# Moving the second quad's queries and keys from GpSimd's casting loads to a hardware queue, more of the early casts to VectorE, and holding GpSimd's loads back

## The chip, the cores and the metric

The kernel runs on one core of one Trainium2 chip. The metric is the time of one execution in device microseconds. A core has TensorE (PE in the profile; its weight loads are PEld), VectorE (DVE), ScalarE (ACT), GpSimd (POOL) and SyncE (SP), and 16 DMA engines which all queues share. Loads issued by SyncE or ScalarE go by hardware queues, and in this kernel they bring float32 as it is into staging tiles. Loads issued by GpSimd can change the type on the way, float32 to float16. The Trainium skill states the same ("DMA: Bandwidth & Descriptors", SWDGE vs HWDGE vs iDMA: a cast during a DMA is GpSimd's alone). That is why a load moved to a hardware queue needs a cast by an engine afterwards.

## The reference

```python
batch, n_heads, seq, head_dim = (8, 12, 448, 64)        # q, k, v, float32
scores = scale * np.matmul(q, k.transpose(0, 1, 3, 2))
m = np.max(scores, axis=-1, keepdims=True)
e = np.exp(scores - m)
attn = e / (np.sum(e, axis=-1, keepdims=True) + np.exp(-m) + 1e-09)
x = attn @ v                                            # then to (3584, 768)
h = x @ w_in                                            # 768 x 2048 ("gemm1" here)
P = a[0] + a[1]*h + a[2]*h**2 + a[3]*h**3
Q = 1.0 + abs(b[0])*abs(h) + abs(b[1])*h**2
out = (P / (Q + 1e-6)) @ w_out                          # 2048 x 768 ("gemm2" here)
```

## The kernel before

Four heads of one batch entry are a "quad"; there are 3 quads per batch entry, 24 in all. For each quad the kernel transposes q and k, multiplies them (scores), takes exps on ScalarE, forms the denominators and the product with v ("attend"), and feeds gemm1, a rational function on VectorE and ScalarE, and gemm2. Batch entry 0 is done in two halves of 224 queries, so that gemm1 can start early.

The program is written as a list of operations in queues. A small planner in the kernel file simulates the engines with estimated durations and fixes each engine's static order from that. Its estimates do not run on the chip; only the order does. Three constants say when the scores of batch entry 1 and later are "due" in that plan:

```python
T0 = 18.0; T1 = 22.0; TLEAD = 5.0
def quad_due(n):
    if n < 2 * NQ:
        return T1 + 8 * P1 * (n - NQ)       # batch entry 1
    return T0 + 8 * PER * (n - NQ)          # later ones
```

Before, only quad 0 came by hardware queues, in pieces, and GpSimd's loads began at once with quad 1:

```python
def piece(ti, pr, jh, nj, dma, lat, cast, late=False):   # ti: k or q; pr: pair of heads; jh: half
    ...                                                  # one DMA into a float32 staging tile, one cast
piece(0, 0, 0, 2, "ACT", 2.8, "ACT")     # k, first pair, first half
piece(1, 0, 0, 2, "SP", 2.65, "DVE")     # q, first pair
piece(0, 0, 2, 2, "ACT", 3.4, "ACT")
piece(1, 1, 0, 2, "SP", 3.9, "DVE")
piece(0, 1, 0, 2, "ACT", 3.6, "ACT")     # k, second pair, first half
piece(0, 1, 2, 2, "SP", 3.7, "ACT")
...
kload.append(load_op(1, k, kn, "k", kfree, NN))          # GpSimd: casting load, 4 heads
qload.append(load_op(1, q, qn, "q", qfree, NN))
loads(0, "v"); loads(2, "kq"); loads(1, "v"); loads(2, "v")
ORDER = "kq3 i kq4 i kq5 v3 i v4 i v5 o kq6 o o o"       # i: a group of w_in, o: one of w_out
```

w_in comes in four groups of three GpSimd loads each. From quad 6 on, q and k are transposed by DMA instead of TensorE.

The softmax here doesn't subtract the row's maximum and nothing guards it: scores larger than these inputs give would overflow.

Of the kernel before, what the change touches and what calls it, by code (L numbers as in the profile page):

```python
# [8 lines left out]
F32 = mybir.dt.float32  # L9
# [149 lines left out]
def kernel(  # L159
# [11 lines left out]
    nc = tc.nc  # L171

    B, H, S, D = q.shape
    DM, FF = moe_w_in.shape
    J = 4
    P = S // J
# [10 lines left out]
    NE, NX, NV, NN, NK, NH, NO, NS = 12, 2, 5, 3, 6, 3, 3, 2  # L187
# [7 lines left out]
    def ring(name, n, shape, dt=F16):  # L195
# [14 lines left out]
    g_sb = ring("g", 2, [128, NFC, S])  # L210
    gx = ring("gx", 2, [128, NFC, 128])

    qn = ring("qn", NN, [P, 4, J, D])
    kn = ring("kn", NN, [P, 4, J, D])
    vn = ring("vn", NV, [P, 4, J, D])
# [19 lines left out]
    plan = Plan({  # L235
        "PE": ("att", "mm", "tr"),
        "ACT": ("head", "c0", "den", "acast", "osb", "e", "rat"),
        "DVE": ("head", "c0", "cpt", "cpt2", "mult", "cast", "wc", "ng"),
        "POOL": ("gx", "perm", "load"),
        "SP": ("x", "out"),  # L240
    }, NGEN)
# [31 lines left out]
    units += [(b, qd, 0, S) for b in range(1, B) for qd in range(NQ)]  # L273
    PER = 1.95
    DUES = (0, 0, 4, 6)
    T0 = 18.0
    T1 = 22.0
    P1 = 1.3
    LEAD = 45.0
    MB = 3  # L280
    NPE = 6
    TLEAD = 5.0
    ACM = 100

    def quad_due(n):
# [4 lines left out]
    qload, kload, vload = [], [], []  # L290
    late_cp = []
    qfree, kfree, v_free = [], [], []
# [5 lines left out]
    def load_op(n, src, dst, name, free, size):  # L298
        b, qd = divmod(n, NQ)

        def emit():
            nc.gpsimd.dma_start(
                out=dst[n % size],
                in_=src[b, 4 * qd:4 * qd + 4].rearrange("h (p j) d -> p h (j d)", j=J),
            )
        return plan.add("load", Op(
            f"ld{name}{n}", "POOL", 0.7, [hist(free, n, size)], emit,
            rel=0.0 if n < 2 * NQ else quad_due(n) - LEAD, kb=448))
# [20 lines left out]
    def first_loads():  # L329


        casts = {}
        stages = [[h_sb[0], h_sb[1]], [h_sb[2], c_sb[0]]]

        def piece(ti, pr, jh, nj, dma, lat, cast, late=False):
            src, dst = ((k, kn), (q, qn))[ti]
            eng = nc.scalar if dma == "ACT" else nc.sync
            stage = (stages[1][1 - pr] if late else stages[pr][ti]).bitcast(F32)[
                0:P, 0:2 * J * D].rearrange(
                "p (h j d) -> p h j d", h=2, j=J)[:, :, (0 if late else jh):][:, :, 0:nj]  # L340
            rows = src[0, 2 * pr:2 * pr + 2].rearrange("h (p j) d -> p h j d", j=J)
            d = plan.add("head" if dma == "ACT" else "x", Op(
                f"ld0{dma}", dma, 0.43,
                [casts[1 - pr, 1, 0], casts[1, 1, 0]] if late else [],
                lambda: eng.dma_start(out=stage, in_=rows[:, :, jh:jh + nj]),
                kb=56 * nj, lat=lat))
            out = (late_q[:, 2 * pr:2 * pr + 2] if late
                   else dst[0][:, 2 * pr:2 * pr + 2, jh:jh + nj])
            c = Op(f"c0{ti}{pr}{jh}", cast, (0.12 if cast == "DVE" else 0.2) + 0.11 * nj, [d],
                   lambda: nc.vector.tensor_copy(out=out, in_=stage) if cast == "DVE"  # L350
                   else nc.scalar.activation(out=out, in_=stage, func=AF.Copy))
            if (ti, pr, jh) != (1, 1, 0):
                plan.add("c0", c)
            for j in range(jh, jh + nj, 2):
                casts[ti, pr, j // 2] = c
        piece(0, 0, 0, 2, "ACT", 2.8, "ACT")
        piece(1, 0, 0, 2, "SP", 2.65, "DVE")
        piece(0, 0, 2, 2, "ACT", 3.4, "ACT")
        piece(1, 1, 0, 2, "SP", 3.9, "DVE")
        piece(0, 1, 0, 2, "ACT", 3.6, "ACT")  # L360
        piece(0, 1, 2, 2, "SP", 3.7, "ACT")
        for pr in range(2):
            piece(1, pr, 2, 2, "SP", 6.8, "DVE", True)
        return casts

    def loads(n, which="kqv"):
        if "k" in which:
            kload.append(load_op(n, k, kn, "k", kfree, NN))
            qload.append(load_op(n, q, qn, "q", qfree, NN))
        if "v" in which:  # L370
            vload.append(load_op(n, v, vn, "v", v_free, NV))

    def transpose_by_pe(n):

        parts, trs = [], []
        nh = 2 if n == 0 else 1
        for pr in range(2):
            ops = [[], []]
            for jh in range(nh):
                for ti, (src, dst, ld) in enumerate(((kn, kt, kload), (qn, qt, qload))):  # L380
                    un = {}
                    late = n == 0 and ti == 1 and jh == 1
                    js = range(J * jh // nh, J * (jh + 1) // nh)

                    def emit(pr=pr, un=un, src=src, js=js, late=late):
                        tp = gen[un["bank"]].bitcast(F16)
                        for j in js:
                            for hh in range(2):
                                nc.tensor.transpose(  # L389
                                    tp[64 * hh:64 * hh + 64, j * P:(j + 1) * P],  # L390
                                    late_q[:, 2 * pr + hh, j - J // 2, :] if late
                                    else src[n % NN][:, 2 * pr + hh, j, :],
                                    ident[0:P, 0:P])

                    def emit_cp(pr=pr, un=un, dst=dst, js=js):
                        c0, c1 = js[0] * P, (js[-1] + 1) * P
                        nc.vector.tensor_copy(
                            out=dst[n % NK][:, pr * S + c0:pr * S + c1],
                            in_=gen[un["bank"]].bitcast(F16)[:, c0:c1])
                    cp = Op(f"cpt{n}", "DVE", 0.1 + 0.24 / nh, [], emit_cp)  # L400
                    src_op = first_casts[ti, pr, jh] if n == 0 else ld[n]
                    tr = Op(f"t{n}", "PE", 0.4 / nh,
                            [src_op, ident_op, hist(qk_free, n, NK)], emit,
                            gen=(True, un, cp), mode="t")
                    trs.append(tr)
                    cp.deps = [tr]
                    if late:
                        late_cp.append(cp)
                    else:
                        plan.add("cpt" if n < NQ else "cpt2", cp)  # L410
                    ops[jh].append(cp)
                    tr.late = late
                    if pr == 1 and not late and (jh == nh - 1 or ti == 1):
                        (kfree, qfree)[ti].append(tr)
            if n == 0 and pr == 0:
                plan.add("cpt", first_casts[1, 1, 0])
            parts.append(ops)
        if n == 2:
            for cp in late_cp:
                plan.add("cpt", cp)  # L420
        qxp.append(None)
        kxp.append(None)
        qk_ready.append(parts)
        return trs
# [303 lines left out]
    first_casts = first_loads()  # L728
# [3 lines left out]
    ab = plan.add("x", Op("ab", "SP", 0.9, [abz], emit_ab, kb=1))  # L732
    babs_op = plan.add("head", Op("babs", "DVE", 0.2, [ab], emit_babs))

    qload.append(None)
    kload.append(None)
    ident_op = plan.add("load", Op("ident", "POOL", 0.6, [], emit_ident))
    kload.append(load_op(1, k, kn, "k", kfree, NN))
    qload.append(load_op(1, q, qn, "q", qfree, NN))
    loads(0, "v")  # L740
    loads(2, "kq")
    loads(1, "v")
    loads(2, "v")
# [18 lines left out]
    first = [op for op in trs[0] if not op.late]  # L762
    late = [op for op in trs.pop(0) if op.late]
    prev = None
    for i in range(len(units)):
        m0 = len(e_ops)
        passes = scores(i)
        nu = units[i + 1] if i + 1 < len(units) else None
        nxt = trs.pop(NQ * nu[0] + nu[1], []) if nu else []
        if nu and nu[0]:  # L770
            for op in nxt:
                op.due = quad_due(NQ * nu[0] + nu[1]) - TLEAD
                plan.add("tr", op)
            nxt = []
        more = {}
        if i == 0:
            more = {-1: first[:2], 0: first[2:4], 1: first[4:], 2: nxt[:1], 3: nxt[1:2]}
            rest = nxt[2:]
        elif i < NQ:
            more = {1: rest, 3: late if i == 2 else nxt}  # L780
            rest = []
        for op in more.get(-1, []):
            plan.add("att", op)
        for t, s in enumerate(passes):
            plan.add("att", s)
            for op in more.get(t, []):
                plan.add("att", op)
            if t == 1:
                for op in prev or []:
                    plan.add("att", op)  # L790
        prev = attend(i, m0)
# [66 lines left out]
```

## Time and profile before

| | value |
|---|---|
| time, median of 3 runs | 432.84 us (432.69 to 432.94) |
| span of the profiled run | 431.5 us (this run took 433.28 us, above all timed ones) |
| TensorE busy, 0 to 27.3 us | 18.81 of 27.3 us |
| TensorE busy, 27.3 to 60 and 60 to 120 us | all of it |
| first gemm1 matmul | 27.30 us |

First, busy time by stretches. The columns are the stretch, its length, then busy time and number of instructions for each engine, the granted TensorE clock, the DMA share and GB/s.

```profile
core 0: us, PE busy (x) PEld busy (x) DVE busy (x) ACT busy (x) POOL busy (x), PEclk, DMA share, GB/s
0.00:16.00 16.00, 8.76 (x128) 5.51 (x128) 4.66 (x28) 8.84 (x13) 9.89 (x19) 1.00 1.07 165
16.00:27.30 11.30, 10.05 (x236) 6.89 (x229) 5.88 (x21) 9.32 (x14) 6.30 (x9) 1.00 1.33 202
27.30:60.00 32.70, 32.70 (x495) 21.74 (x494) 24.29 (x44) 31.02 (x40) 15.78 (x24) 1.00 1.26 203
60.00:120.00 60.00, 60.00 (x512) 30.13 (x510) 57.20 (x80) 52.95 (x60) 27.09 (x35) 1.00 1.10 145
```

From 27.3 to 120 us TensorE has no gap, and from there to 400 us only 0.5 us, so only the head (and a tail of about 3 us) can be shortened. In the last column GpSimd's casting loads are counted by the float16 bytes they write; they read twice that. (The page of the profile has 22.35 MB for GpSimd's queue, and 45.62 MB read from memory in all.)

Next, lines of the timeline: start, duration, engine, line, operation, and in brackets the idle time before it and what ended it.

```profile
1.49 0.83 POOL L302 DMA_DIRECT2D kn<-in_k_dram  x1 [0.18 <-issue]
7.56 0.72 ACT L351 ACTIVATE kn<-h 112x256 f16<-112x256 f32 x2 [2.74 <-DMA h<-in_k_dram]
8.36 0.56 PE L472 MATMUL sps<-qt,kt 64*128 64x224 f16 x4
14.65 1.71 PE L507 MATMUL gen<-e,vn 112*32 112x224 f16 x32
20.13 0.94 PE L507 MATMUL gen<-e,vn 112*32 112x224 f16 x32
27.30 0.75 PE L573 MATMUL gen<-x,w_in 128*128 128x224 f16 x6
```

GpSimd issues its first load at 1.49 us. The last early pieces of quad 0 (k of the second pair of heads) are cast only at 7.56 us, and the scores that need them start at 8.36. The same 32 matmuls take 1.71 us at 14.65 us and 0.94 us at 20.13 us, though the granted clock column reads 1.00: TensorE runs slowly at first. ScalarE works in a fixed order: the first pair's scores are computed from 4.95 us on, but the first exp starts only at 8.19 us.

```profile
8.19 1.70 ACT L480 ACTIVATE e<-sps 112x896 f16<-112x896 f32 x2
```

The chain of waits gives the wait for that piece of k (start, duration, what):

```profile
1.72 5.82 DMA h<-in_k_dram
```

### The profile page before, as it was taken

The page shows a single profiled execution, that of the slowest core. Times are in us where ns is not written, and L with a number is a line of the kernel's source. Part 1 is how long each engine was busy: PE and PEld are TensorE (multiplying, and loading weights), DVE is VectorE, ACT ScalarE, POOL GpSimd, SP SyncE. Part 2 cuts the span into 40 slices and gives each one's busy share as a digit, 9 for nine tenths or more (in the row PEclk, how much of TensorE's full clock was granted, in tenths as well). Part 3 has the DMA queues.
Part 4 walks back from the last instruction along what each step waited for, and adds up shares of the span by engine and source line. Part 5 has one row for each costly group of instructions (what it writes and reads, how often), then busy time and mean ns, then how long its engine had stood idle before and what let it go on. Part 6 is the DMA issues. An engine that isn't in the chain of part 4 may idle for free.

```text
span 431.5 us, 8834 instructions
## 1 busy us (share of the span) xinstructions
PE 419.2 (97%) x3680; PEld 218.7 (51%) x3680; DVE 339.9 (79%) x505; ACT 327.8 (76%) x386; POOL 120.7 (28%) x172
## 2 busy tenths in 40 slices
PE   3999999999999999999999999999999999999996
PEld 2667665544444444444454444444444455555563
DVE  2445999998999887698998668979698788999800
ACT  4699999798888777888886897877798854578521
POOL 5655516566005340423703333052000000000000
PEclk9999999999999999999999999999999999999999
DMA  9999999899606947299399886373211011111132
GB/s 148 202 200 205 207 180 150 152 154 162 123 2 69 160 85 118 28 141 115 58 117 107 119 123 85 81 108 73 45 36 38 2 36 38 36 38 36 39 103 81
DMA packets 78153, 43.12 MB, mean 100 GB/s; under 512 B 36128, under 2 KB 74528, under 8 KB 78112
## 3 DMA queue, kind: packets, MB, share of 16 engines
q0 software_dynamic: 37856, 22.35, 39.7%
q1 hardware_dynamic: 39472, 19.80, 25.5%
q8 instruction: 29, 0.48, 0.5%
q10 hardware_dynamic: 784, 0.39, 0.4%
q14 instruction: 12, 0.10, 0.1%
HBM read 45.62 MB, written 11.01 MB: 131 GB/s over the span
## 4 chain that ended last, share of the span: by engine, by line
PE 89%; ACT 4%; DMA 3%; DVE 1%; issue 1%; ACTq 0%; POOLq 0%
PE gen L671 34%; PE gen L573 33%; PE gen L507 12%; PE sps L472 10%; DMA kn<-in_k_dram 2%; ACT e L480 2%; DMA h<-in_k_dram 1%; ACT c L625 1%; ACT c L628 1%; PE gen L389 1%; DVE h L590 0%; ACT lden L521 0%; DVE x L535 0%; ACT lden L523 0%; DVE c L614 0%
## 5 line engine op out<-in xcount | busy, mean ns | idle before, releaser
L480 ACT ACTIVATE e<-sps 112x896 f16<-112x896 f32 x192 | 167.1, 917 | 41.5 <-PE sps L472 41.1
L573 PE MATMUL gen<-x,w_in 128*128 128x448 f16 (+1 forms) x864 | 161.8, 332 | 0.0
L671 PE MATMUL gen<-w_out,g 128*128 128x384 f16 (+2 forms) x768 | 135.9, 326 | 0.0
L573 PEld LDWEIGHTS <-w_in 128*128 128x128 f16 x864 | 79.9, 98 | 68.3 <-issue 14.4
L671 PEld LDWEIGHTS <-g 128*128 128x128 f16 x768 | 72.7, 98 | 58.4 <-issue 10.4
L590 DVE CAST h<-gen 128x448 f16<-128x448 f32 x113 | 69.4, 618 | 24.4 <-PE gen L573 24.3
L614 DVE TENSOR_TENSOR n<-n,h 128x1792 f16<-128x1792 f16 x64 | 70.1, 1095 | 0.7
L625 ACT ACTIVATE c<-c,oneeps_c 128x1792 f16<-128x1792 f16 x32 | 57.3, 1791 | 11.4 <-DVE c L614 11.1
L472 PE MATMUL sps<-qt,kt 64*128 64x448 f16 (+1 forms) x432 | 58.4, 343 | 2.3 <-ACT e L480 1.1
L648 POOL COPY gx<-g 128x1024 f16<-128x1024 f16 x8 | 8.3, 1040 | 183.1 <-DVE g L614 183.1
L693 ACT ACTIVATE o<-gen 128x384 f32<-128x384 f32 (+2 forms) x56 | 27.4, 490 | 36.2 <-PE gen L671 36.0
L628 ACT ACTIVATE c<-c 128x1792 f16<-128x1792 f16 x32 | 54.6, 1705 | 0.3
L610 DVE TENSOR_SCALAR n<-n,abc 128x1792 f16<-128x1792 f16 x64 | 44.3, 693 | 1.1
L614 DVE TENSOR_TENSOR g<-n,c 128x1792 f16<-128x1792 f16 x32 | 35.1, 1098 | 12.8 <-ACT c L628 11.5
L433 POOL COPY kp<-kn 112x256 uint32<-112x256 uint32 x36 | 26.1, 755 | 57.2 <-DMA kt<-kp 50.3
L507 PE MATMUL gen<-e,vn 112*32 112x448 f16 (+1 forms) x864 | 41.8, 337 | 0.0
L535 DVE TENSOR_TENSOR x<-gen,lden 128x448 f16<-128x448 f32 (+1 forms) x54 | 28.3, 563 | 13.9 <-ACT lden L523 12.7
L614 DVE TENSOR_TENSOR c<-c,w 128x1792 f16<-128x1792 f16 x32 | 35.2, 1100 | 0.0
L472 PEld LDWEIGHTS <-kt 64*128 64x128 f16 x432 | 15.0, 96 | 36.5 <-issue 32.9
L507 PEld LDWEIGHTS <-vn 112*32 112x32 f16 x864 | 23.1, 99 | 14.0
L433 POOL COPY qp<-qn 112x256 uint32<-112x256 uint32 x36 | 25.2, 726 | 18.1 <-DMA qt<-qp 18.0
L610 DVE TENSOR_SCALAR n<-h,abc 128x1792 f16<-128x1792 f16 x32 | 24.7, 772 | 0.1
(42 smaller groups left out, 248.1 us busy)
## 6 DMA issues: line engine op xcount, KB each, us to landing
vn<-in_v_dram POOLq DMA_DIRECT2D x24, 224.0 KB, 8.5
kn<-in_k_dram POOLq DMA_DIRECT2D x23, 224.0 KB, 5.7
qn<-in_q_dram POOLq DMA_DIRECT2D x23, 224.0 KB, 7.4
w_in<-in_moe_w_in_dram POOLq DMA_DIRECT2D x12, 256.0 KB, 9.7
w_out<-in_moe_w_out_dram POOLq DMA_DIRECT2D x4, 768.0 KB, 16.2
out_dram<-o SPq DMA_DIRECT2D x8, 336.0 KB, 3.2
out_dram<-o SPq DMA_DIRECT2D x8, 288.0 KB, 2.8
out_dram<-o SPq DMA_DIRECT2D x7, 240.0 KB, 2.5
```

What stands on the lines that cost most here:

```text
L433: nc.gpsimd.tensor_copy(out=mid[0].bitcast(U32)[:, pr], in_=src[n % NN].bitcast(U32)[:, 2 * pr:2 * pr + 2] .rearrange("p e j d -> p j e d"))
L472: nc.tensor.matmul(out=sps[m % NS][0:(P if i == 0 and j == 1 else 128), hh, ci * qw:(ci + 1) * qw], lhsT=kt[n % NK][r, c0:c0 + (P if i == ...
L480: nc.scalar.activation(out=e_sb[m % NE], in_=sps[m % NS][0:P, :, 0:S], func=AF.Exp, scale=scale)
L507: nc.tensor.matmul(out=gen[unit["bank"]][32 * h:32 * h + 32, 0:qw], lhsT=lhs(h, j), rhs=e_sb[m % NE][:, h % 2, c0:c0 + qw], start=(j == 0) ...
L535: mult.emit = lambda s=s, uu=uu: nc.vector.tensor_tensor(out=x_sb[b % NX][:, 2 * qd + s, q0:q0 + qw], in0=gen[uu["bank"]][:, 0:qw], in1=ld ...
L573: nc.tensor.matmul(out=gen[unit["bank"]][:, fi * qw:(fi + 1) * qw], lhsT=w_in_sb[wg][:, c // 2, c % 2, (fc % FG) * 128:(fc % FG + 1) * 128 ...
L590: nc.vector.tensor_copy(out=dst, in_=src)
L610: return lambda: nc.vector.tensor_scalar(out=out, in0=in0, scalar1=s1, scalar2=s2, op0=op0, **kw)
L614: return lambda: nc.vector.tensor_tensor(out=out, in0=in0, in1=in1, op=ALU.mult)
L625: lambda: nc.scalar.activation(out=c, in_=c, func=AF.Ln, bias=oneeps_c)))
L628: lambda: nc.scalar.activation(out=c, in_=c, func=AF.Exp, scale=-1.0)))
L671: nc.tensor.matmul(out=gen[unit["bank"]][:, 0:wd], lhsT=lhs, rhs=w_out_sb[f][:, fc % FG, cols], start=(fc == 0), stop=(fc == NFC - 1))
```

## The change

The intent: the first quad's pieces should have the DMA engines to themselves, so that the exps start sooner. Quad 1's q and k also come by SyncE's queue, in four larger transfers into a part of a tile that is still unused, and VectorE casts them. VectorE also takes over the two casts of quad 0's last k pieces, which ScalarE did before. A tiny memset of v's tile by VectorE (`vz`), placed behind the casts of quad 0, keeps GpSimd from issuing its first load before those casts. The due times are adjusted.

```diff
-    T0 = 18.0
-    T1 = 22.0
+    T0 = 17.0
+    T1 = 24.0
-    TLEAD = 5.0
+    TLEAD = 1.0
...
-        piece(1, 1, 0, 2, "SP", 3.9, "DVE")
-        piece(0, 1, 0, 2, "ACT", 3.6, "ACT")
-        piece(0, 1, 2, 2, "SP", 3.7, "ACT")
+        piece(0, 1, 1, 0, 2, "SP", 3.3)
+        piece(0, 0, 1, 0, 2, "ACT", 3.3)
+        piece(0, 0, 1, 2, 2, "SP", 3.4)
         for pr in range(2):
-            piece(1, pr, 2, 2, "SP", 6.8, "DVE", True)
+            for ti in range(2):
+                piece(1, ti, pr, 0, 4, "SP", 3.9)        # quad 1, VectorE casts
...
+                    for key in ((0, 1, 1, 0), (0, 0, 1, 0), (0, 0, 1, 1)):
+                        plan.add("cpt", first_casts[key])
+                    plan.add("cpt", vz)
...
-    kload.append(load_op(1, k, kn, "k", kfree, NN))
-    qload.append(load_op(1, q, qn, "q", qfree, NN))
+    vz = Op("vz", "DVE", 0.06, [first_casts[0, 1, 1, 0]],
+            lambda: nc.vector.memset(vn[0][:, 0, 0, 0:2], 0.0))
     loads(0, "v")
+    vload[0].deps.append(vz)
```

(The second set of arguments of `piece` has the quad in front. Some bookkeeping is cut.) "Sixth piece" below means `piece(0, 0, 1, 0, ...)`, k of the second pair, first half: the third issue on ScalarE's queue.

More of the change, by code (lines that the diff above doesn't have):

```diff
@@ L333, in first_loads, with piece @@
         stages = [[h_sb[0], h_sb[1]], [h_sb[2], c_sb[0]]]
-        def piece(ti, pr, jh, nj, dma, lat, cast, late=False):
+        more = g_sb[1].rearrange("p f s -> p (f s)").bitcast(F32)
+        def piece(n, ti, pr, jh, nj, dma, lat, cast="DVE", late=False):
             src, dst = ((k, kn), (q, qn))[ti]
             eng = nc.scalar if dma == "ACT" else nc.sync
-            stage = (stages[1][1 - pr] if late else stages[pr][ti]).bitcast(F32)[
-                0:P, 0:2 * J * D].rearrange(
-                "p (h j d) -> p h j d", h=2, j=J)[:, :, (0 if late else jh):][:, :, 0:nj]
-            rows = src[0, 2 * pr:2 * pr + 2].rearrange("h (p j) d -> p h j d", j=J)
+            size = 2 * J * D
+            if n:
+                stage = more[0:P, (2 * pr + ti) * size:(2 * pr + ti + 1) * size]
+            else:
+                stage = (stages[1][1 - pr] if late else stages[pr][ti]).bitcast(F32)[
+                    0:P, 0:size]
+            j0 = 0 if late else jh
+            stage = stage.rearrange("p (h j d) -> p h j d", h=2, j=J)[:, :, j0:j0 + nj]
+            h0 = 4 * n + 2 * pr
+            rows = src[0, h0:h0 + 2].rearrange("h (p j) d -> p h j d", j=J)
             d = plan.add("head" if dma == "ACT" else "x", Op(
                 f"ld0{dma}", dma, 0.43,
-                [casts[1 - pr, 1, 0], casts[1, 1, 0]] if late else [],
+                [casts[0, 1 - pr, 1, 0], casts[0, 1, 1, 0]] if late else [],
                 lambda: eng.dma_start(out=stage, in_=rows[:, :, jh:jh + nj]),
@@ L347, in piece @@
             out = (late_q[:, 2 * pr:2 * pr + 2] if late
-                   else dst[0][:, 2 * pr:2 * pr + 2, jh:jh + nj])
-            c = Op(f"c0{ti}{pr}{jh}", cast, (0.12 if cast == "DVE" else 0.2) + 0.11 * nj, [d],
-                   lambda: nc.vector.tensor_copy(out=out, in_=stage) if cast == "DVE"
+                   else dst[n][:, 2 * pr:2 * pr + 2, jh:jh + nj])
+            c = Op(f"c{n}{ti}{pr}{jh}", cast, (0.12 if cast == "DVE" else 0.2) + 0.11 * nj,
+                   [d], lambda: nc.vector.tensor_copy(out=out, in_=stage) if cast == "DVE"
                    else nc.scalar.activation(out=out, in_=stage, func=AF.Copy))
-            if (ti, pr, jh) != (1, 1, 0):
-                plan.add("c0", c)
             for j in range(jh, jh + nj, 2):
-                casts[ti, pr, j // 2] = c
-        piece(0, 0, 0, 2, "ACT", 2.8, "ACT")
-        piece(1, 0, 0, 2, "SP", 2.65, "DVE")
-        piece(0, 0, 2, 2, "ACT", 3.4, "ACT")
-        piece(1, 1, 0, 2, "SP", 3.9, "DVE")
-        piece(0, 1, 0, 2, "ACT", 3.6, "ACT")
-        piece(0, 1, 2, 2, "SP", 3.7, "ACT")
+                casts[n, ti, pr, j // 2] = c
+            return c
+        plan.add("c0", piece(0, 0, 0, 0, 2, "ACT", 2.8, "ACT"))
+        plan.add("c0", piece(0, 1, 0, 0, 2, "SP", 2.65))
+        plan.add("c0", piece(0, 0, 0, 2, 2, "ACT", 3.4, "ACT"))
+        piece(0, 1, 1, 0, 2, "SP", 3.3)
+        piece(0, 0, 1, 0, 2, "ACT", 3.3)
+        piece(0, 0, 1, 2, 2, "SP", 3.4)
         for pr in range(2):
-            piece(1, pr, 2, 2, "SP", 6.8, "DVE", True)
+            for ti in range(2):
+                piece(1, ti, pr, 0, 4, "SP", 3.9)
+        for pr in range(2):
+            plan.add("c0", piece(0, 1, pr, 2, 2, "SP", 6.8, "DVE", True))
         return casts
@@ L378, in transpose_by_pe @@
             ops = [[], []]
+            if n == 1:
+                for ti in range(1 - pr, 2):
+                    plan.add("cpt", first_casts[n, ti, pr, 0])
             for jh in range(nh):
+                if n == 0 and pr == 0 and jh == 1:
+                    for key in ((0, 1, 1, 0), (0, 0, 1, 0), (0, 0, 1, 1)):
+                        plan.add("cpt", first_casts[key])
+                    plan.add("cpt", vz)
+                if n == 0 and pr == 1 and jh == 1:
+                    plan.add("cpt", first_casts[1, 0, 0, 0])
                 for ti, (src, dst, ld) in enumerate(((kn, kt, kload), (qn, qt, qload))):
@@ L400, in transpose_by_pe @@
                     cp = Op(f"cpt{n}", "DVE", 0.1 + 0.24 / nh, [], emit_cp)
-                    src_op = first_casts[ti, pr, jh] if n == 0 else ld[n]
+                    src_op = first_casts[n, ti, pr, jh] if n < 2 else ld[n]
                     tr = Op(f"t{n}", "PE", 0.4 / nh,
@@ L414, in transpose_by_pe @@
                         (kfree, qfree)[ti].append(tr)
-            if n == 0 and pr == 0:
-                plan.add("cpt", first_casts[1, 1, 0])
             parts.append(ops)
@@ L733 @@
     babs_op = plan.add("head", Op("babs", "DVE", 0.2, [ab], emit_babs))
-    qload.append(None)
-    kload.append(None)
+    qload += [None] * 2
+    kload += [None] * 2
     ident_op = plan.add("load", Op("ident", "POOL", 0.6, [], emit_ident))
-    kload.append(load_op(1, k, kn, "k", kfree, NN))
-    qload.append(load_op(1, q, qn, "q", qfree, NN))
+    vz = Op("vz", "DVE", 0.06, [first_casts[0, 1, 1, 0]],
+            lambda: nc.vector.memset(vn[0][:, 0, 0, 0:2], 0.0))
     loads(0, "v")
+    vload[0].deps.append(vz)
     loads(2, "kq")
@@ L776 @@
         if i == 0:
-            more = {-1: first[:2], 0: first[2:4], 1: first[4:], 2: nxt[:1], 3: nxt[1:2]}
+            more = {-1: first[:2], 0: first[2:5], 1: first[5:], 2: nxt[:1], 3: nxt[1:2]}
             rest = nxt[2:]
```

## The prediction

> **What bounds the kernel now.** Span 431.5 us. The busy time by windows shows TensorE busy 32.70 of 32.70 us from 27.3 to 60 us and almost all of it up to 400 us; from 0 to 27.3 us it is busy 18.81 us. So TensorE is the limit after the first gemm1 matmul (27.30 us in the timeline); only the head (8.5 us idle) and the tail (about 3 us) have slack. What starts the TensorE-full stretch earlier comes off the total, one for one. The head also runs cold: 8 transposes take 0.59 us until about 17.9 us, later 0.39; 32 attend matmuls 1.71, later 0.94. The granted clock reads 1.00 throughout, so this is not in that column. The Trainium skill ("TensorE: Matmul & The Clock Gate", Part 1) says the array runs at half rate until some 3.4 us of sustained activity; the trace agrees: warm 5.7 us after gaps end at 12.18 us.
>
> **Head, before.** The waits show TensorE's transposes waiting 6.2 us for ScalarE's casts of k; the chain of waits has 5.82 us of DMA into the staging tile (1.72 to 7.54). That third piece of k shares the DMA engines with GpSimd's casting loads, issued from 1.49 us and moving from 4 us. Scores of the second head pair start only at 8.36, the exps at 8.19. Exps 8 to 11 start at 19.65, mults end about 27, gemm1 starts at 27.30. ScalarE is full from 20 us.
>
> **What the change does.**
> - Removes GpSimd's loads of quad 1 (2 issues, 1.5 us of GpSimd) and delays all its loads until a memset behind the fifth or sixth early cast: about 6 us instead of 1.49.
> - The six early pieces have the DMA engines to themselves. Alone, hardware-queue data moved at about 300 GB/s (DMA view, 2.5 to 4 us), so 0.69 MB is in by about 4.7 us, against 7.54. Gain there: 2.5 to 3 us.
> - Quad 1: four 224 KB pieces, estimated 3 us more, in at about 7.5 us. Four casts of twice the columns, at 0.28 to 0.55 us for the present ones: 2.5 to 4 us of VectorE, which is only 30% busy in the first 15 us. ScalarE loses two casts (0.8 us).
> - Against it: a DMA hole. GpSimd's first data came 2.5 us after its first issue, so v0 flows from 8.5 us, with a hole of about 1 us after quad 1, and a slow ramp (115 GB/s at 4 to 6 us before). v0 lands near 10.5, quad 2 near 13, w_in0 near 23, as now: bytes in flight are not less. The first w_in bounds gemm1's start at about 23 us, so at most 4 us can be won.
>
> **On the critical path.** Exps start near 5.5 us instead of 8.2, quad 2's near 15 instead of 19.65, TensorE warms some us earlier. I expect gemm1 at 24 to 25.5 us and a gain near 3 us; some is lost to the changed order and to w_in1, w_in2 having less slack (now 4 to 5 us). T0, T1, TLEAD reorder batch 1; small either sign.
>
> **Predicted:** 429.9 us, range 427.8 to 432.3; faster by over 2% 0.02, within 0.965, slower 0.015.
>
> **Right or wrong in the profile.** Right: first exp at 5 to 6 us; no wait of 2 us for a cast of k; attend matmuls at 0.94 us for 32 before 17 us; first gemm1 matmul at 24 to 25.5 us; TensorE full after; rest unchanged. Wrong: VectorE's in-order casts delaying the copies of transposes; TensorE waiting on v0 or k2 at 10 to 14 us; gemm1 starting no earlier than 27 because w_in0 lands late; new TensorE gaps at 28 to 60 us.

## The result

The changed kernel took 433.47 us (median of 6 runs, 432.37 to 434.33); the kernel before took 432.68 us beside it (6 runs, 431.95 to 432.94). The ratio is 1.002, 95% interval 1.0001 to 1.0039: the same at the 2% mark, and if anything a little slower. Ratios here are the mean time of one kernel's fast runs over that of the other's in the same rounds, so they are not quite the ratio of the medians quoted.

The spread is wider than before, 2 us instead of 1. The profiled run of this section took 434.18 us, one of the slower ones; a second profile (run a_again, 432.94 us) is used as well.

Busy time by the same stretches, after:

```profile
0.00:16.00 16.00, 9.85 (x144) 6.12 (x144) 6.68 (x38) 8.76 (x12) 8.22 (x16) 1.00 0.91 173
16.00:27.30 11.30, 10.03 (x238) 6.67 (x242) 4.60 (x16) 10.66 (x16) 5.67 (x8) 1.00 1.37 199
27.30:60.00 32.70, 31.34 (x475) 20.13 (x464) 24.40 (x45) 30.44 (x39) 17.46 (x24) 1.00 1.26 204
60.00:120.00 60.00, 59.51 (x512) 30.29 (x511) 57.91 (x79) 51.91 (x58) 25.07 (x35) 1.00 1.07 147
```

The head did more (16 more TensorE instructions by 16 us). But TensorE now has gaps where it had none: 1.36 us between 27.3 and 60 us, 0.49 us between 60 and 120 us. Timeline lines that answer to those of before:

```profile
6.73 0.49 DVE L357 CAST kn<-h 112x256 f16<-112x256 f32 x2 [1.56 <-DMA h<-in_k_dram]
7.54 1.04 POOL L302 DMA_DIRECT2D vn<-in_v_dram  x1 [6.23 <-DVE kt L416]
7.59 0.62 PE L489 MATMUL sps<-qt,kt 64*128 64x224 f16 x4
25.42 0.91 PE L590 MATMUL gen<-x,w_in 128*128 128x224 f16 x6
```

The first exp now starts at once when its scores are there:

```profile
5.61 0.92 ACT L497 ACTIVATE e<-sps 112x896 f16<-112x896 f32 x1 [0.94 <-PE sps L489]
```

That is not the work of the gate. In every trace of the changed kernel and of its variants the first exp starts between 5.53 and 5.70 us, whether the sixth piece is cast at 5.38 or at 8.59 us; what it no longer waits for is the late casts in ScalarE's order.

The sixth piece is cast at 6.73 us, 0.83 us earlier than before. GpSimd issues its first load at 7.54 us, 6 us later than before. Gemm1 starts at 25.42 us, 1.88 us earlier. Later on, TensorE's timeline has these three gaps, and the summary of its waits (in total, times, longest) names them:

```profile
43.30 0.37 PE L590 MATMUL gen<-x,w_in 128*128 128x224 f16 x2 [0.22 <-DMA w_in<-in_moe_w_in_dram]
44.62 0.36 PE L590 MATMUL gen<-x,w_in 128*128 128x224 f16 x2 [0.96 <-DMA w_in<-in_moe_w_in_dram]
69.22 0.56 PE L489 MATMUL sps<-qt,kt 64*128 64x448 f16 x4 [0.49 <-DMA qt<-qp]
```

```profile
PE gen L590 <- DMA w_in<-in_moe_w_in_dram: 1.2, 2, 1.0
PE sps L489 <- DMA qt<-qp: 0.5, 1, 0.5
```

At 43 us it is the fourth group of w_in; at 69 us the first q that is transposed by DMA. None of these waits is in the profile before. Why are these loads late? Queue by queue, what had moved by 16 us, before:

```profile
q0 software_dynamic: 3486, 1.73, 82.7%
q1 hardware_dynamic: 1200, 0.57, 15.6%
q10 hardware_dynamic: 720, 0.34, 9.0%
```

and after:

```profile
q0 software_dynamic: 1892, 0.94, 48.4%
q1 hardware_dynamic: 2160, 1.49, 35.2%
q10 hardware_dynamic: 720, 0.34, 7.3%
```

The second number is MB. The hardware queues move float32, GpSimd's (q0) counts half of what it reads. In bytes read, before had 2 x 1.73 + 0.57 + 0.34 = 4.37 MB by 16 us, after 2 x 0.94 + 1.49 + 0.34 = 3.71 MB. The deficit of 0.66 MB is worth 1.6 us at 0.4 MB/us (200 GB/s in the last column, from 16 to 60 us, means about 0.4 MB read per microsecond), and the stream is full until about 60 us, so it is not made up before the late loads are needed. The last load of w_in was issued at 32.9 us before, and at 34.83 us after. The deficit is not the same in every run: in the second profile of the same kernel (a_again) the count is 4.09 MB, a deficit of 0.28 MB or 0.7 us, and the last load of w_in was issued at 33.2 us.

A rough account of the profiled run: gemm1 starts 1.88 us earlier; an estimated 0.7 us of that is only reordered, because 340 TensorE instructions came before it instead of 356 (two transposes of 8 matmuls fewer, 0.36 to 0.39 us each); the new gaps to 120 us are 1.85 us. That leaves 1.88 - 0.7 - 1.85 = -0.7 us. The measured shift of the first matmul on the tile gx of gemm2 is 169.1 to 169.9 us, so -0.8 us. (The section on why the prediction was wrong has a sum over all runs, which puts the reordering at 0.3 to 0.4 us.)

There is a second cause, the order. After 72 gemm1 matmuls of 224 columns TensorE turns to the fourth w_in group. In the timeline before that was at 48.07 us, now at 42.72 us, for the adjusted due times put gemm1 ahead of batch entry 1's attention, and gemm1 starts 1.88 us earlier.

```profile
48.07 0.75 PE L573 MATMUL gen<-x,w_in 128*128 128x224 f16 x6
42.72 0.37 PE L590 MATMUL gen<-x,w_in 128*128 128x224 f16 x2
```

So TensorE asks 5.35 us earlier for a group that is loaded 2 us later. In a_again it asks at 41.98 us, 6.1 us earlier, and the load is issued only 0.3 us later; it still waits 1.0 us. The earlier demand uses up most of the slack, and what is left decides whether a late stream shows.

### The profile page after: what moved, and what is told of

It reads as the page before. It is cut to its first block, busy times and chain, and to the rows that moved or that the text cites. A ratio compares the mean times of both kernels' runs of the same rounds, so it can differ in the third digit from the quotient of the medians.

```text
span 432.4 us, 8838 instructions
## 1 busy us (share of the span) xinstructions
PE 419.1 (97%) x3680; PEld 218.1 (50%) x3680; DVE 343.8 (79%) x512; ACT 328.3 (76%) x384; POOL 117.0 (27%) x170
## 4 chain that ended last, share of the span: by engine, by line
PE 79%; DMA 14%; ACT 3%; DVE 2%; POOL 1%; issue 1%; ACTq 0%; POOLq 0%
PE gen L688 33%; PE gen L590 28%; PE gen L524 10%; PE sps L489 8%; DMA w_in<-in_moe_w_in_dram 5%; DMA qn<-in_q_dram 4%; DMA qt<-qp 4%; DMA h<-in_k_dram 1%; ACT e L497 1%; ACT c L642 1%; ACT c L645 1%; DVE h L607 0%; POOL qp L450 0%; DVE x L552 0%; POOL vn L302 0%
## 5 line engine op out<-in xcount | busy, mean ns | idle before, releaser
L627 DVE TENSOR_SCALAR n<-n,abc 128x1792 f16<-128x1792 f16 x64 | 45.3, 708 | 1.1
L450 POOL COPY kp<-kn 112x256 uint32<-112x256 uint32 x36 | 21.2, 621 | 58.5 <-DMA kt<-kp 49.8
```

What stands on the lines that cost most here:

```text
L450: nc.gpsimd.tensor_copy(out=mid[0].bitcast(U32)[:, pr], in_=src[n % NN].bitcast(U32)[:, 2 * pr:2 * pr + 2] .rearrange("p e j d -> p j e d"))
L627: return lambda: nc.vector.tensor_scalar(out=out, in0=in0, scalar1=s1, scalar2=s2, op0=op0, **kw)
```

## The experiments

All timed runs gave correct results within the reference's tolerance. Unless said otherwise, the edits keep every engine's instruction order as in the changed kernel, which was compared instruction by instruction; what moves is only when something may start. The theories: (S) supply: holding GpSimd back makes the whole load stream late, and it binds later. (C) crowding: the first quad's sixth piece does not have the DMA engines to itself, for quad 1's transfers run beside it. (O) order: the due times set what TensorE asks for and when, whatever the loads do.

**a_again: the changed kernel again.** No edit.

> The changed kernel once more, unaltered, as a yardstick on the same chip and to see whether its times fall into two clusters (432.4 to 432.9 and 434.0 to 434.3 in the first six). Supply theory (the load stream runs 1.6 to 1.8 us late because GpSimd issues its first load at 7.54 us, so TensorE later waits on w_in and on the first transposed q): the trace again shows 1 us or more of waits on w_in near 43 us. If the waits vary from run to run, times vary with them. Expected 432.4 to 434.4, ratio near 1.002.

Measured: 433.41 us (432.94 to 434.12), ratio 1.0025. In this profile the sixth piece was cast at 6.03 us, GpSimd issued at 6.84 us, gemm1 started at 24.98 us, and TensorE still waited 1.0 us on w_in and 0.2 us on the transposed q. So gemm1 was 2.3 us earlier than before and the span 431.0 us against 431.5. The moment at which the sixth piece lands varies by 0.7 us between runs, and the gate passes this on to all GpSimd's loads. No two clear clusters; the spread stays.

**a_nogate: GpSimd not held back.**

```diff
-            lambda: nc.vector.memset(vn[0][:, 0, 0, 0:2], 0.0))
+            lambda: None)
```

> The changed kernel with all instructions in the same order, but without the memset that holds back GpSimd's first load: loads begin near 1.5 us. Supply theory: w_in's last group and the transposed q land 1.5 us or more earlier, the 1.2 us and 0.5 us waits go, and the time falls by 1 us or more (below 432.3), unless the first quad's pieces, now sharing the DMA engines, land later than 6.7 us and give the same back in the head. Crowding rival (GpSimd's stream is what hurts the first quad): sixth piece lands after 8 us, gemm1 starts 1 us or more later, time over 434.

Measured: 433.76 us (432.92 to 434.03), ratio 1.0026. GpSimd issued at 1.50 us. The waits on w_in and on the transposed q were gone (none in the list after 27 us but 0.4 us on ScalarE), as S has it. But the head lost as much:

```profile
7.59 0.50 DVE L357 CAST kn<-h 112x256 f16<-112x256 f32 x2 [2.37 <-DMA h<-in_k_dram]
27.16 0.75 PE L590 MATMUL gen<-x,w_in 128*128 128x224 f16 x6
```

The sixth piece was cast at 7.59 us and gemm1 started at 27.16 us. This is the exception that the expectation allowed for S, a loss in the head that gives the gain back; of the rival's three signs only the later gemm1 came. The first exp was at 5.54 us here too, so an early first exp did not by itself bring gemm1 forward. The gate does its work in the head, and it is paid for later.

**a_swap: the sixth piece goes ahead of quad 1 in SyncE's queue.**

```diff
-        piece(0, 0, 1, 0, 2, "ACT", 3.3)
-        piece(0, 0, 1, 2, 2, "SP", 3.4)
+        piece(0, 0, 1, 0, 2, "SP", 3.3)
+        piece(0, 0, 1, 2, 2, "ACT", 3.4)
```

> The changed kernel, same order on every engine, only the sixth piece (k of the second pair, first half) goes by SyncE's queue ahead of quad 1, and the piece with its second half by ScalarE's. Crowding-by-quad-1 theory: that piece, which landed at 6.70 us because SyncE's four quad 1 transfers share the DMA engines, lands near 5 us, scores of the second pair start near 6 us instead of 7.59, GpSimd's gate may open earlier, and the head gains 0.5 to 1.5 us. Rival (pieces 5 and 6 simply wait for bytes): landing of the later of the two stays near 6.7 us and nothing moves, under 0.3 us.

Measured: 432.02 us (431.42 to 432.77), ratio 0.9994; 1.4 us under a_again of the same rounds, median against median.

```profile
5.38 0.56 DVE L357 CAST kn<-h 112x256 f16<-112x256 f32 x2 [0.30 <-DMA h<-in_k_dram]
6.25 0.98 POOL L302 DMA_DIRECT2D vn<-in_v_dram  x1 [4.94 <-DVE kt L416]
24.33 0.75 PE L590 MATMUL gen<-x,w_in 128*128 128x224 f16 x6
```

The two casts start at 5.38 us, the gate opens at 6.25, gemm1 starts at 24.33 us: now 3 us earlier than before, inside what the prediction said. Still only 1.3 us of the span are won (430.2 against 431.5), with 0.6 us waited on w_in and 0.4 us on the transposed q. Part of the gain comes through the gate, since GpSimd starts earlier too, so this run alone does not split C from S.

**a_q1small: quad 1's transfers a quarter of the size.** Wrong on purpose (the rest of the staging is zeros; it passed the tolerance all the same).

```diff
+            ns = 1 if n else nj
-                lambda: eng.dma_start(out=stage, in_=rows[:, :, jh:jh + nj]),
+                lambda: (n and nc.gpsimd.memset(stage[:, :, 1:], 0.0),
+                         eng.dma_start(out=stage[:, :, 0:ns], in_=rows[:, :, jh:jh + ns])),
```

> Wrong on purpose: the changed kernel with quad 1's four transfers cut to a quarter of their bytes (the rest of their staging is filled by GpSimd while it waits), every engine's order otherwise the same. Crowding theory: the sixth piece, cast at 6.73 and 6.03 us in two profiles of the changed kernel because quad 1's transfers share the DMA engines, is cast by about 5 us or earlier, as the prediction had it (4.7); the gate opens 1 to 1.7 us earlier. Rival (the piece is late for a reason of its own, such as being ScalarE's third issue): still later than 5.6 us.

Measured: 432.62 us (431.99 to 434.35), ratio 0.9996 [0.9975, 1.0016].

```profile
5.75 0.50 DVE L357 CAST kn<-h 112x256 f16<-112x256 f32 x2 [0.51 <-DMA h<-in_k_dram]
```

The sixth piece was cast at 5.75 us, so the expectation for C (5 us or earlier) was missed. How much the crowding costs, this run can't say. Five traces have the full transfers and the same early loads, and in them the cast starts at 5.58 (a_T0TLold), 5.84 (a_olddues), 6.03 (a_again), 6.07 (a_T1old) and 6.73 us (the first profile): 5.75 lies among them. Nor did the edit free the DMA engines as meant: the packets became smaller, not fewer, and from 2 to 6 us SyncE's queue still took 54% of the engines' time, against 57 to 72% in the five.

That quad 1's data does run beside the first quad's is seen in the DMA view. By 6.6 us, before the cast at 6.73, SyncE's queue had moved 0.86 MB, of which only 0.34 MB are the first quad's. By 4.7 us the two hardware queues had moved 0.66 MB (0.78 in a_again), close to the 0.69 that the prediction asked for; but not all of it was the first quad's, and a piece can be used only when its last packet is in. ScalarE's queue had ended 640 of its 720 packets by 4.7 us and the last between 6.2 and 6.5 us (in a_again 708, and the last between 5.3 and 5.6 us).

**a_gate1: the gate opens after the first q cast.** The memset is moved behind the cast of `(0, 1, 0, 0)`.

```diff
+  # in the VectorE cast of a piece:
+  (n, ti, pr, jh) == (0, 1, 0, 0) and nc.vector.memset(vn[0][:, 0, 0, 0:2], 0.0)
-            lambda: nc.vector.memset(vn[0][:, 0, 0, 0:2], 0.0))
+            lambda: None)
```

> The changed kernel without the swap, the gate moved to after the first q cast (GpSimd issues near 3.8 us instead of 7.54). Supply theory: the late waits on w_in and transposed q go (gain up to 1.5 us), but the sixth piece, still behind quad 1's, is slowed by GpSimd's data only if it lands after about 6.3 us, when that data starts; expected 432.0 to 433.0, between the changed kernel and the swap with the early gate. If the time equals the changed kernel's (433.4), the stream's start is not what costs.

Measured: 431.95 us (431.51 to 432.13), ratio 0.9983 [0.9971, 0.9996]. GpSimd issued at 3.94 us; no wait on w_in or on the transposed q; the sixth piece was cast at 6.47 us, between the two values of the changed kernel. The fourth w_in group is asked for at 42.09 us, as early as in the changed kernel, and is there:

```profile
3.94 0.83 POOL L302 DMA_DIRECT2D vn<-in_v_dram  x1 [2.63 <-DVE vn L357]
25.09 0.75 PE L590 MATMUL gen<-x,w_in 128*128 128x224 f16 x6
42.09 0.75 PE L590 MATMUL gen<-x,w_in 128*128 128x224 f16 x6
```

By 16 us 4.33 MB had been read, as in the kernel before (4.37). This is S with nothing else moved. It is slightly faster than the kernel before, and at the 2% mark the same.

**a_swapgate1: both edits.**

> The swap of pieces 5 and 6 kept, and GpSimd's gate moved from after both k casts (it issued at 6.25 us with the swap) to after the first q cast, about 3.8 us; every engine's order otherwise the same. Supply theory: GpSimd's data joins before quad 1's transfers end, the dip of the DMA rate near 9 us goes, w_in's last group and the first transposed q land 1 us or more earlier, the waits of 0.6 and 0.4 us go, and the time is 431.0 to 431.6 (0.5 to 1 us under the swap alone). Rival (the waits are a matter of order, or the earlier stream slows quad 1 and the first quad as much as it helps): same as the swap alone within 0.3 us, or slower with gemm1 later than 24.8 us.

Measured: 431.46 us (431.01 to 432.22), ratio 0.9975 [0.9961, 0.9989]. The wait on w_in was gone, that on the transposed q was 0.7 us:

```profile
66.50 0.55 PE L489 MATMUL sps<-qt,kt 64*128 64x448 f16 x4 [0.66 <-DMA qt<-qp]
```

**a_swaplate: a later gate, an edit that failed.** It was meant to put the memset behind quad 1's first q cast, with the swap.

> The dose the other way: swap kept, the gate after quad 1's first q cast, so GpSimd issues about 1.6 us later than with the swap (near 7.9 us). Supply theory: w_in's last group and the transposed q land about 1.6 us later, the waits grow from 1.0 to 2.5 us or more, the time rises by 1 to 2.5 us to 433 or more. Rival (supply has slack): within 0.4 us of the swap.

Measured: 433.82 us (433.48 to 435.01), ratio 1.0032. The number looks like a hit but is void: the memset stood behind the load in the program, so it held nothing back. GpSimd issued from 1.5 us on, the memset waited for the load instead (it started at 11.85 us on VectorE) and zeroed a few values of v in one head, which the tolerance let pass. What it does show: with GpSimd early, the sixth piece is late even with the swap (cast at 8.59 us).

**a_swaplag: the dose done properly.** With the swap, GpSimd fills v's tile twice before its first load.

```diff
+            n == 0 and name == 'v' and [nc.gpsimd.memset(vn[0], 0.0) for _ in range(2)]
             nc.gpsimd.dma_start(out=dst[n % size], ...)
```

> The dose done properly, since the edit of a_swaplate failed: its memset came after the load of v in the program, so it held nothing back (GpSimd issued at 1.5 us) and zeroed two columns of v besides. Here the swap is kept with the change's gate, and GpSimd fills the v tile twice before its first load, which puts all its loads about 1.5 to 2 us later than with the swap (6.25 us), every engine's order otherwise the same. Supply theory: waits on w_in's last group and on the transposed q grow from 1.0 us to 2 us or more and the time rises by 1 to 2 us over the swap's 432.0. Rival (supply has slack): within 0.4 us.

Measured: 434.47 us (434.38 to 435.6), ratio 1.0054.

```profile
6.32 1.96 POOL L302 MEMSET vn<- 112x1024 f16 x2 [5.01 <-DVE vn L756]
8.58 0.83 POOL L302 DMA_DIRECT2D vn<-in_v_dram  x1 [0.30 <-POOL vn L302]
```

2.3 us of lag came with 2.45 us more than the swap alone. The place was not where S has it: the late waits stayed at 0.6 us each, and the loss came in the head, where TensorE now waited 1.0 us on k, 0.8 us on q and 0.3 us on v, and gemm1 started at 26.52 us. Nor is this dose clean. The memsets ran beside a cast of quad 1's k on VectorE and stretched it to 1.22 us (0.42 us in a_swap), and TensorE waited 0.7 us on that cast at 8.61 us:

```profile
7.33 1.22 DVE L357 CAST kn<-g 112x512 f16<-112x512 f32 x1 [0.53 <-DMA g<-in_k_dram]
```

So part of the loss belongs to the edit, and the size is no proof of S.

**a_best1 and a_best2: quad 6's k and q loaded ahead of the first w_out group**, to take away the last wait. Both have the swap; a_best1 the gate after the first cast, a_best2 after the second q cast, `(0, 1, 1, 0)`.

```diff
-    ORDER = "kq3 i kq4 i kq5 v3 i v4 i v5 o kq6 o o o"
+    ORDER = "kq3 i kq4 i kq5 v3 i v4 i v5 kq6 o o o o"
```

> Swap, gate after the first q cast, and k, q of quad 6 loaded ahead of the first w_out group instead of behind it (one place in GpSimd's order; all other engines the same). Supply theory: the last wait, 0.7 us on the first transposed q near 66 us, goes, and the time is 0.3 to 0.7 us under that of the swap with early gate (431.46), so 430.7 to 431.2. Rival (the next limit takes over at once): no change, 431.3 to 431.7.

> As a_best1, with the gate one cast later (after the second pair's q, GpSimd issuing near 5.1 us instead of 3.9). Head theory: GpSimd's first data arrives about 2.5 us after the issue, so after the sixth piece has landed; that piece lands near 5.3 us instead of 6.1 and the second pair's scores start near 6.2 instead of 7.2. Supply theory: the stream is about 1 us later. If the two weigh the same, the time equals a_best1's within 0.3 us; if the head weighs more, it is 0.3 to 0.8 us lower.

Measured: 431.66 us (430.95 to 432.37), ratio 0.9981, and 431.68 us (430.37 to 432.14), ratio 0.9977. The wait on the transposed q went, as expected, and both profiles had 0.6 us of waiting on w_in instead. The expected 0.3 to 0.7 us did not come. GpSimd issued at 3.95 and 5.55 us; between these two positions of the gate there is no difference.

**a_warm: seven matmuls on constants in TensorE's idle time before the first transposes**, otherwise as a_best1. The clock theory: the early matmuls are slow (32 attend matmuls 1.71 us, later 0.94) until TensorE has been busy for a while, and that delays the head.

> As a_best1, with seven matmuls on constants ahead of the first transposes, in TensorE's idle time from about 1.2 to 3.9 us. Clock theory [...]: 8 transposes take 0.39 us instead of 0.59 from before 10 us on (now from about 14 us), 32 attend matmuls 0.94 instead of 1.3 to 1.7, gemm1 starts 0.5 to 1.5 us earlier, the time falls by 0.5 to 1.5 us unless supply binds again. Rival (the head waits on DMA and ScalarE, not on TensorE's speed): same within 0.3 us.

Measured: 431.35 us (431.06 to 431.93), ratio 0.9977: same as without. The premise failed, for TensorE did not speed up earlier:

```profile
1.43 2.77 PE L405 MATMUL sps<-w,ones 128*32 128x448 f16 x7 [1.43 <-DVE kt L258]
12.88 1.71 PE L524 MATMUL gen<-e,vn 112*32 112x224 f16 x32
18.02 0.94 PE L524 MATMUL gen<-e,vn 112*32 112x224 f16 x32
```

The attend matmuls at 12.88 us still took 1.71 us. So the run says nothing on what a warm TensorE would be worth; that stays open.

**a_olddues, b_newdues: the due times alone.** The changed kernel with 18, 22, 5; the kernel before with 17, 24, 1. Here the order of all engines changes, since the planner runs anew.

> The changed kernel with T0, T1 and TLEAD as before (18, 22, 5). Order theory: these numbers put batch 1's scores later and gemm1 earlier, so TensorE asks for w_in's last group at 42.7 us instead of 49.2 us; with the old values the wait on w_in goes and the time falls by 1 us or more. Supply theory: the stream is as late as before, so a wait turns up elsewhere (k, q or v of batch 1), and the time stays within 0.7 us of the changed kernel's.

> The kernel before with only T0, T1 and TLEAD of the change (17, 24, 1). If those three numbers are a gain or a loss by themselves, it shows here without the loads: order theory (they move gemm1 ahead of attention, so TensorE runs into w_in) expects 433.5 to 435 with waits on w_in; if they merely suit the earlier head, 432.3 to 433.5; if they are a pure gain hidden in the change, under 432.

Measured: 441.27 us (438.86 to 443.76), ratio 1.0205, and 441.94 us (441.83 to 443.56), ratio 1.0225. The first has an interval of 1.0178 to 1.0231, so at the 2% mark it is unclear; the second is slower. Neither time was as expected. In a_olddues the waits on w_in and on the transposed q did go, as the order theory had it, but other waits took their place. The old values do not mend the changed kernel, they cost it 7.9 us more; the new values cost the kernel before over 9 us. In a_olddues most of the loss lies between 65 and 80 us; busy time by stretches there, and TensorE's waits between 50 and 80 us:

```profile
65.00:70.00 5.00, 3.62 (x22) 1.43 (x21) 5.00 (x8) 5.00 (x7) 1.24 (x2) 1.00 1.68 147
70.00:75.00 5.00, 3.72 (x42) 1.65 (x45) 4.93 (x6) 5.00 (x7) 4.51 (x6) 0.80 1.33 187
75.00:80.00 5.00, 3.73 (x30) 1.26 (x22) 3.98 (x6) 4.51 (x7) 2.08 (x2) 0.86 1.51 188
```

```profile
PE sps L489 <- ACT e L497: 3.9, 5, 1.8
```

ScalarE and VectorE are full, TensorE waits 3.9 us on exps, and its granted clock falls to 0.80. By 60 us this kernel had done 177 gemm1 matmuls against 133 (144 in a_again) in the changed kernel, and only 224 attend matmuls with v against 256. I read this as gemm1 going ahead and its rational function filling VectorE and ScalarE while the exps wait; no run takes that apart. b_newdues shows the same waits on exps between 60 and 120 us (4.0 us), but not all of its loss was traced.

**a_T1old, a_T0TLold: one part of the due times set back.**

> The changed kernel with T1 alone set back to 22 (T0 17, TLEAD 1 kept). If T1, which dates the scores of batch 1's quads, is what the order hangs on, this alone gives most of the 8 us that all three gave (439 to 442), with TensorE waiting on ScalarE's exps near 65 to 80 us; if not, 432 to 435.

> The changed kernel with T0 and TLEAD set back to 18 and 5 and T1 kept at 24. The counterpart: if T1 carries the 8 us, this stays at 432 to 435; if T0 or TLEAD does, 438 or more; if any of the three by itself upsets the order, both this run and the one before are slow.

Measured: 437.99 us (436.24 to 438.57), ratio 1.0118, and 435.97 us (434.76 to 437.32), ratio 1.0079. Against the changed kernel's 433.4 us that is 4.6 and 2.6 us, so a_T1old fell between its two ranges, and of the three alternatives for a_T0TLold the last came, both runs slow: no single constant carries the loss. The two nearly add up to the 7.9 us of both, but this may be chance, for the late waits differ: in a_T1old 2.5 us on the transposed q, in a_T0TLold 1.6 us on an exp. What is shown is the crossing of a_olddues and b_newdues: each set of values does well with its own loads and costs 8 to 10 us with the other.

## Why the prediction was wrong

1. *TensorE is the limit after the first gemm1 matmul; what starts that stretch earlier comes off the total, one for one.* **This is the step that failed.** It was true of the kernel before, whose profile has no TensorE wait on a load after 27.3 us. It did not follow that it stays true. The prediction saw the load stream's limit only at the first group of w_in ("near 23, as now") and gave the later groups a slack of 4 to 5 us. In fact the new order and the earlier head asked for the last group 5.35 us earlier (42.72 against 48.07 us; 6.1 us in a_again), and the held-back stream issued it 0.3 to 2 us later, having lost 0.28 to 0.66 MB (0.7 to 1.6 us) by 16 us. The slack was gone, and 1.85 us of new gaps appeared (1.4 us in a_again), against a gain of 1.88 us (2.32 us) in the head. a_gate1 shows it from the other side: an earlier gate alone, same order, took the waits on loads away and 1.5 us off the time.
2. *First exps near 5.5 us, gemm1 at 24 to 25.5 us.* Right in the numbers: 5.61 us, and 25.42 and 24.98 us in two profiles. For the first exp this was partly luck. The prediction had it follow from the early pieces landing sooner, but a_nogate, where the sixth piece was cast at 7.59 us, has it at 5.54 us as well: it came from the casts that left ScalarE's order. And not all of the earlier gemm1 was gain, for two transposes were put off to later.
3. *The six early pieces have the DMA engines to themselves and are in by 4.7 us.* Wrong, mis-sized by 1.3 to 2 us: cast at 6.03 to 6.73 us. The rate was about right; the exclusive use was not, for quad 1's transfers are issued from 2.18 us and run beside them. The Trainium skill says as much ("DMA: Bandwidth & Descriptors", Issuing engines are not separate DMA queues): DMAs from all engines "interleave with each other". Runs agree: 0.5 MB of quad 1's data had moved by 6.6 us, before the cast at 6.73 us, and with GpSimd's loads let in early the cast came at 7.59 us (a_nogate) and 8.59 us (a_swaplate). With the piece ahead in SyncE's queue it came at 5.38 us. How much of the delay is due to quad 1 alone is not shown.
4. *GpSimd's loads start about 6 us, with a hole and a slow ramp.* Right in kind, too small: 6.84 and 7.54 us, because the gate waits for the late piece. The same error counted twice, in the head and in the stream.
5. *VectorE's casts take 2.5 to 4 us.* Too large: 0.42 to 0.58 us for each of quad 1's four, 0.28 to 0.29 for quad 0's. They were not what delayed anything.
6. *T0, T1, TLEAD: small either sign.* Wrong: 7.9 and over 9 us in the two crossed runs.
7. *TensorE warms some us earlier.* Half right: in the profiled run 32 attend matmuls took 1.63 us at 13.51 us and 0.94 us at 18.39 us. The trace has this at other times in each run. The forecast of 0.94 us before 17 us was missed. The prediction's own figure for the kernel before, 5.7 us, is longer than the 3.4 us that it quotes; see the last section.

One sum holds for the whole family. Take the start of gemm1, add TensorE's idle time from there to 120 us, and look how much later the first gemm2 matmul on the tile gx comes. In ten traces with the changed kernel's TensorE order this is 142.05 to 142.13 us (a_again, a_nogate, a_gate1, a_swap, a_swapgate1, a_swaplate, a_swaplag, a_best1, a_best2, a_warm), in the kernel before 141.76. So what the variants differ by up to there is these two terms, the head and the gaps after it, and the reordering costs 0.3 to 0.4 us. Two traces, the changed kernel's first profile (142.61) and a_q1small (142.73), lose half a microsecond more, and where it goes was not traced.

What the gate trades can be read from runs with one order (the last of them with the stretched cast). Without the swap: GpSimd's first issue at 1.50 us gave 433.76 us, at 3.94 us 431.95 us, at 6.84 to 7.54 us 433.41 us. With it: 3.92 us gave 431.46 us, 6.25 us 432.02 us, 8.58 us 434.47 us. Too early, GpSimd's stream delays the first quad; too late, the stream is late. The best is between: near 4 us it is worth 0.25% over the kernel before (a_swapgate1), and 5.55 us did as well in a_best2. So holding GpSimd back for a moment paid; the change's gate stood too late.

Left open: what the slow early TensorE costs, and why 0.6 to 0.7 us of waiting on one load or another came back in each of the better versions.

## What to carry to other kernels

When a load is held back so that an urgent one gets through, count the bytes that the DMA engines will not have moved, turn them into microseconds at the measured rate, and look for the consumer far downstream that had less slack than that, counted from the moment at which the new order asks for it. Open a gate before the urgent transfers end, not after they have been consumed: here 4 to 5.5 us did better than 7. In a statically ordered kernel, constants that shape the order belong to the arrival times they were tuned for: test a change of loads with its order frozen, and the order by itself.

## What the Trainium skill lacked or had wrong

- "TensorE: Matmul & The Clock Gate", Part 1, gives a warm-up budget of about 3.4 us of sustained work, on a free-running window. In these runs TensorE turned fast 3.1 us (a_best1) to about 7 us (a_swaplate, with one gap of 0.27 us in between) after its last gap of 0.4 us or more. For planning, one to two windows is closer than one. (Seven matmuls of 448 columns from 1.43 to 4.2 us did not advance it in a_warm, but they lasted 2.77 us, less than the budget.)
- "DMA: Bandwidth & Descriptors" has a latency to the first byte, but no figure for how fast GpSimd's stream gets going after it. In the changed kernel, after the first issue at 7.54 us, the core's DMA moved 130 GB/s at 10 to 12 us, 140 at 12 to 14 and 168 at 14 to 16, against 200 later.
- "SBUF — State Buffer", SBUF: two separate sides, says that VectorE and GpSimd lock each other out of a shared port. It gives no size for a case like this one. Beside GpSimd's memset of v, VectorE's cast of 112x512 took 1.22 us (a_swaplag, at 7.33 us) against 0.42 us without it (a_swap, at 6.55 us), which agrees. Beside GpSimd's issues of loads it is less regular: the cast of 112x256 took 0.55 us in the kernel before (at 3.28 us), but 0.28 us in the changed kernel at 13.21 us, while GpSimd issued from 12.96 to 14.37 us.
